# Attention and two MLPs on one core: weight copies on another queue, a denser operand split, and another pace of small work

## The chip, the cores and the metric

The kernel runs on one core of a Trainium2 chip. The metric is the device time of one execution in microseconds (us). TensorE (PE) multiplies, with its weight loads shown as PEld; VectorE (DVE) and ScalarE (ACT) do the elementwise work; GpSimd (POOL) and SyncE (SP) issue most of the transfers. Each engine runs its instructions in the order in which the program emits them.

## The reference

All data is float32. Softmax attention with a tanh cap over 4 batches, 12 heads, 448 tokens and head dimension 64 gives x (1792 x 768). A first MLP follows, then a second, gated one with two more products:

```
scores = cap * tanh(q k^T / 8 / cap);  attn = exp(scores - max) / sum
x = concat_heads(attn v)                       # 1792 x 768
x = square(relu(x @ w_in)) @ w_out             # 768 -> 2048 -> 768
h = ((x @ w1) * (x @ w2)) @ w3                 # 768 -> 1024 -> 1024
out = h @ w_out2                               # 1024 -> 768
```

The MLP weights come as float64 words, are narrowed on the chip, and are split into a high and a low part so that a product is three TensorE products: high by high, high by low, low by high.

## The kernel before, in words

**Attention (lines 393 to 713).** One loop, `for u in range(NU + 10)`, with `NU` = 84, emits everything. Each u below 84 is one unit: a 128-key slice of a pair of heads p (24 pairs, 7 units for two pairs). At an even u two units get their scores (`emit_qk`, tile `sc`) and `tanh`; `emit_exp` works on unit u-1, `emit_sum` adds unit u-4 into the denominators on DVE, and at an odd u `emit_pv` multiplies units u-5 and u-4 with v (tile `pv`). A table `later` says at which u a pair's `pv` is copied to `acc` (`evacuate`, line 515: pair 21 at u = 83, pair 22 at 87, pair 23 at 89), at which u its denominators are summed by TensorE (`emit_den`: pairs 20 and 21 at u = 83, pairs 22 and 23 at 91) and stored (`store_den`, line 520: u = 85 and 93).

**Weights beside the attention.** `w_piece` (line 561) is a generator, advanced once per u, that narrows and splits one piece of a weight. The eight "w0" pieces belong to the first MLP's first block; two steps after its low part is formed (line 80), such a piece is copied from SBUF to DRAM (`w0_d`, shown as `w_d`) by two transfers (line 580). `w_products` multiplies w3 with the last weight on TensorE; `w_store` sends the result out (line 610). At the first even u at which all of that is emitted, u = 84, the loop closes the weights' SBUF pool `wq`. The x operands (`xs[0]`, `xs[1]`, shown as x0h, x0l, x1h, x1l) are allocated in the same place; an operand waits only for the old tile it overlaps. Still at u = 84, three raw weight pieces are fetched and the eight w0 pieces read back (line 687), all on SP's queue.

**The hand-over.** `side` holds the generator `splits()`: for batch 0, then batch 1, `split_x` (line 273) makes in seven steps the high parts on ACT (line 280) and the low parts on DVE (line 80). It is advanced once per u. After batch 0 is split, each odd u takes one step of `fill`, which is `first_unit`: `front` for two 128-column blocks of w_in (18 products each, with relu, square and split on ACT and DVE), then `back` (six outputs). What is left of `side` and `fill` when the loop ends is emitted then:

```python
            advance(side)
            advance(norms)
        assert not w_open
        while side:
            advance(side)
        for _ in fill:
            pass
```

`normalise` (line 286, in the list `norms`, a step per u) divides a group of pairs by its denominators: it reads the stored denominators back (`dt`), forms reciprocals on DVE, stores them (`rec_d`), spreads them over partitions (`spread`, two transfers per pair into `bs`, line 303) and multiplies `acc` (line 311). For the last batch the last group is pairs 22 and 23.

**First MLP (lines 866 on).** 16 units of `front` and `back`, all products on TensorE, with weight conversion beside them. Batch 3's operand is split in the third unit and first used by the fourth.

**Second MLP.** 16 steps s, eight per pair of batches. `front2` (line 783) makes seven products p(0) to p(6) and combines them on DVE (lines 799, 802); `back2` (line 826) makes 12 outputs y and adds each to `acc` on DVE (line 842). The order in a step is the first half of `front2` (p(0) to p(3)), half of the previous `back2`, the rest of `front2`, the other half. Small work, the sums and splits of operands, waits in the list `duties` and is emitted by `tick(n)`, n items at a time: `tick(2)` after each p(j), `tick(1)` after each y. At s = 2 and s = 6 sums for the second pair are queued (16 and 3 items), at s = 7 its six operand splits (42 items: three high parts on ACT, three low parts on DVE and one empty item each).

Of the kernel before, what the change touches and what calls it, by code (L numbers as in the profile page):

```python
# [9 lines left out]
F32 = mybir.dt.float32  # L10
# [11 lines left out]
def tile_kernel(ctx, tc, q, k, v, cap, w_in, w_out, w1, w2, w3t, wo2, out):  # L22
# [31 lines left out]
    GD = 2  # L54
# [230 lines left out]
    def normalise(b, n0, n1, lags):  # L285

        rows = slice(2 * n0, 2 * n1)
        dt_ = stat.tile([128, 4 * GD * S // 128], F32, name="dt", bufs=2)[:, :2 * (n1 - n0) * S // 128]  # L290
        POOL.dma_start(out=dt_, in_=den_d[b][rows].rearrange("h s -> (h s)").rearrange("(p f) -> p f", p=128))
        for _ in range(lags[0]):
            yield
        DVE.scalar_tensor_tensor(out=dt_, in0=dt_, scalar=1e-9, in1=dt_, op0=ALU.mult, op1=ALU.add)
        DVE.reciprocal(out=dt_, in_=dt_)
        POOL.dma_start(out=rec_d[b][rows].rearrange("h s -> (h s)").rearrange("(p f) -> p f", p=128), in_=dt_)
        rs = {}

        def spread(n):
            if n < n1:  # L300
                rs[n] = cv.tile([128, 2, HW], F32R, name="bs", bufs=2).bitcast(F32).rearrange("p t n -> p (t n)")[:, :S]
                for j in range(2):
                    POOL.dma_start(out=rs[n][j * D:(j + 1) * D], in_=rec_d[b][2 * n + j].partition_broadcast(D))

        spread(n0)
        spread(n0 + 1)
        for n in range(n0, n1):
            for _ in range(lags[1] if n == n0 else lags[2]):
                yield
            a = acc[b][:, n, :]  # L310
            DVE.tensor_tensor(out=a, in0=a, in1=rs.pop(n), op=ALU.mult)
            normal.add((b, n))
            spread(n + 2)
# [75 lines left out]
    with ExitStack() as actx:  # L389
# [125 lines left out]

        def evacuate(p):
            b, hp = divmod(p, NP)
            DVE.tensor_copy(acc[b][:, hp, :], pvs.pop(p))

        def store_den(p):  # L520
            b, g, n = den_group(p)
            if p % NP // 2 == g + n - 1:
                stg = ap_.tile([128, S], F32, name="stg", bufs=1)
                DVE.tensor_copy(stg, dens.pop(b))
                for i in range(4):
                    POOL.dma_start(out=den_d[b].rearrange("(n i) s -> n i s", i=4)[g:g + n, i, :],
                                   in_=stg[32 * i:32 * i + n])
                lags = (6, 4, 3) if b < B - 1 else (7, 3, 1) if n == GD else (4, 3, 1)
                norms.append(normalise(b, 2 * g, 2 * (g + n), lags))
# [30 lines left out]
        def w_piece(n):  # L560
            kind, i, z = wsrc[n]
            raw = wraw.pop(n)
            if kind == "wo":
                x = block() if i < 5 else wq.tile([128, 2, HW], F32R, name=f"wo{i}{z}")
                parts = [x[:, 0, :], x[:, 1, :]]
            else:
                nj = raw.shape[-1] // 128
                tiles = [wq.tile([128, 3, 128], F32R, name=f"w3{s}", bufs=W3)[:, :nj, :] for s in "hl"]
                parts = [x.rearrange("p a c -> p (a c)") for x in tiles]
            g = narrow(raw, *parts, on=ACT if n >= ON_POOL and n % 2 else DVE, first=POOL if n < ON_POOL else ACT, pool=wq)  # L570
            next(g)
            w_fetch(n + 3)
            for _ in range(LAG):
                yield
            yield from g
            yield
            yield
            if kind == "w0":
                for s, x in enumerate(parts):
                    POOL.dma_start(out=w0_d[i, z, :, s, :], in_=x.bitcast(F32))  # L580
                w3_done.add(wsrc[n])
            else:
                w_ready[wsrc[n]] = parts if kind == "wo" else tiles
# [68 lines left out]
        for u in range(NU + 10):  # L652
            if u < NU and u % 7 in (1, 4):
                load_v(what(u)[0] + 1)
            if 0 <= u - 1 < NU:
                emit_exp(u - 1)
            if u % 2 == 0:
                if u < NU:
                    for x in (u, u + 1):
                        emit_qk(x)  # L660
                    for x in (u, u + 1):
                        emit_tanh(x)
                if w_open:
                    todo = -(-products_left // max((W_END - u) // 2, 1)) if u > W_EVEN else 4
                    for _ in range(todo):
                        x = next(wprod, None)
                        if not x:
                            break
                        products_left -= 1
                    if products_left <= 0:  # L670
                        for _ in wprod:
                            pass
                    if products_left <= 0 and not w_full and not chains:
                        wctx.close()
                        xp = ctx.enter_context(tc.tile_pool(name="x0", bufs=1, side="right", reuse_waits="tile"))
                        for b in range(EARLY):
                            xs[b] = [xp.tile([128, NP, S], F32R, name=f"x{b}{s}") for s in "hl"]
                        new_gtiles(xp)
                        rtiles.extend(cv.tile([128, S], F32, name="cvx", bufs=6) for _ in range(2))
                        w_open = False  # L680
                        fill = first_unit(spare_bank)
                        for _ in range(3):
                            fetch_next()
                        for i in range(2 * FC):
                            halves = [block() for _ in range(2)]
                            for z, x in enumerate(halves):
                                SP.dma_start(out=x.bitcast(F32), in_=w0_d[i, z])
                            wts[i] = [w for x in halves for w in columns(x)]
                        side.append(splits())
            else:  # L690
                w_store()
                if split_done:
                    next(fill, None)
                for x in (u - 5, u - 4):
                    if 0 <= x < NU:
                        emit_pv(x)
                for f in later.pop(u, ()):
                    f()
            for f in later.pop(u, ()):
                f()  # L700
            if w_open and u > 1 and wnext < len(wsrc) and wnext < min(u, W_FAST) * W_RATE[0] + max(u - W_FAST, 0) * W_RATE[1] and w_may_start(wnext):
                chains.append(w_piece(wnext))
                wnext += 1
            advance(chains)
            if 0 <= u - 4 < NU:
                emit_sum(u - 4)
            advance(side)
            advance(norms)
        assert not w_open
        while side:  # L710
            advance(side)
        for _ in fill:
            pass

# [68 lines left out]
    def front2(s):  # L783

        pair = s // NM
        ws = wblk.pop(s)
        ps = [ps_h.tile([128, 512], F32, name="h")[:, :S] for _ in range(7)]
        p1, u2, u3 = (cv.tile([128, S], F32, name="bt", bufs=3) for _ in range(3))
        u4 = spare[1]

        def p(j):
            assert (pair, ORDER[j]) in there
            products(ps[j], ws[j], *place(pair, ORDER[j]))
            if s == NM - 1 and j < 6:
                operand(1, ("B11", "T2", "T3", "B21", "T4", "B22")[j])
            tick(2)

        def add(t, j, u):
            DVE.tensor_tensor(out=t, in0=ps[j], in1=u, op=ALU.add)  # L799

        def gate(j, x, y):
            DVE.tensor_tensor(out=x, in0=x, in1=y, op=ALU.mult)  # L802
            gh, gl = (t[:, s % 2, :] for t in gtiles[j])
            ACT.activation(gh, x, AF.Copy)  # L804
            late.append((gl, x, gh))

        p(0)
        ACT.activation(p1, ps[0], AF.Copy)
        flush()
        p(1)  # L810
        add(u2, 1, p1)
        p(2)
        add(u3, 2, u2)
        p(3)
        add(u4, 3, u3)
        add(u2, 3, u2)
        yield
        p(4)
        add(p1, 4, p1)
        p(5)  # L820
        add(u3, 5, u3)
        gate(0, p1, u3)
        p(6)
        add(u2, 6, u2)
        gate(1, u2, u4)
        yield

    def back2(s):
# [3 lines left out]
        for half in range(2):  # L832
            for j, o in product(range(2), range(half * KB, (half + 1) * KB)):
# [8 lines left out]
                    DVE.tensor_tensor(out=a, in0=y, in1=a, op=ALU.add)  # L842
                if o == half * KB + 1:
                    flush()
                tick(1)
                if m == NM - 1:
                    SP.dma_start(out=out[o * 128:(o + 1) * 128, b * S:(b + 1) * S], in_=a)
            yield
# [117 lines left out]
```

## Time and profile before

| what | value |
|---|---|
| runs of before | 1062.25, 1063.03, 1065.13 us; median 1063.03 us |
| the profiled execution | 1064.73 us; its span 1062.8 us |
| PE busy | 1036.2 us, 97% of the span |
| DVE, ACT, POOL busy | 785.3, 535.2, 198.8 us |
| chain that ended last | PE 86%, DVE 8%, ACT 3%, DMA 1% |

Busy time is a share of the whole span; a stage is read from the rows of its own stretch. Times in rows count from the span's start. In the timeline a row gives start, length, engine, line, output and input; brackets give the idle time just before it and what ended it, as far as the profile can infer. The matmul rows overlap: the time between two starts is the pace, not the length of one.

### The profile page before, as it was taken

How to read it: one execution, taken by the hardware profiler on the slowest of the kernel's cores; microseconds unless marked ns; L12 is line 12 of the kernel's file. 1: busy time of each engine (PE TensorE's matmuls, PEld its weight loads, DVE VectorE, ACT ScalarE, POOL GpSimd, SP SyncE). 2: the span in 40 equal slices, each digit the busy share in tenths (PEclk: the TensorE clock that was granted, in tenths of full speed). 3: DMA queues.
4: the chain of work that ended last, by engine and by line, in shares of the span. 5: the costliest groups of instructions: out<-in, count | busy, mean ns of one | idle time of the engine just before them, and what ended most of it. 6: DMA issues, size and time to landing. Idle time of an engine off the chain costs nothing.

```text
span 1062.8 us, 14544 instructions
## 1 busy us (share of the span) xinstructions
PE 1036.2 (97%) x5136; PEld 844.9 (79%) x5136; DVE 785.3 (74%) x1485; ACT 535.2 (50%) x946; POOL 198.8 (19%) x360
## 2 busy tenths in 40 slices
PE   7999999997999999999999999999999999999998
PEld 2333555554899999999999999999989997999997
DVE  5999988766576878888788787567386678456666
ACT  7899988873776565555666555441311022300100
POOL 3222223324101011111111101002211322131110
PEclk9999999998999999999999999999999999999999
DMA  6667666663245565655656555126554567566443
GB/s 207 180 176 217 192 191 199 206 212 103 77 117 175 172 174 180 191 182 167 179 178 193 179 166 161 45 57 182 166 177 149 175 211 224 163 206 193 137 149 119
DMA packets 74216, 178.69 MB, mean 168 GB/s; under 512 B 10368, under 2 KB 25760, under 8 KB 74144
## 3 DMA queue, kind: packets, MB, share of 16 engines
q0 software_dynamic: 36992, 97.01, 28.9%
q1 hardware_dynamic: 37008, 80.76, 25.9%
q8 instruction: 40, 0.66, 0.3%
q14 instruction: 32, 0.26, 0.1%
q10 hardware_dynamic: 144, 0.00, 0.0%
HBM read 137.45 MB, written 40.28 MB: 167 GB/s over the span
## 4 chain that ended last, share of the span: by engine, by line
PE 86%; DVE 8%; ACT 3%; DMA 1%; issue 1%; POOL 0%; SPq 0%; DVEq 0%
PE h L320 13%; PE h L318 13%; PE h L319 13%; PE y L318 10%; PE y L319 10%; PE y L320 10%; PE sc L438 3%; PE pv L487 3%; PE h L596 2%; PE h L598 2%; PE h L597 2%; DVE sum L468 1%; ACT pt L458 1%; DVE acc L842 1%; ACT pt L454 1%
## 5 line engine op out<-in xcount | busy, mean ns | idle before, releaser
L319 PE MATMUL y<-gl,wb 128*128 128x448 f32 x372 | 136.4, 367 | 0.0
L320 PE MATMUL y<-gh,wb 128*128 128x448 f32 x372 | 136.3, 367 | 0.0
L318 PE MATMUL y<-gh,wb 128*128 128x448 f32 x372 | 136.3, 366 | 0.0
L799 DVE TENSOR_TENSOR bt<-h,bt 128x448 f32<-128x448 f32 x96 | 59.8, 623 | 91.8 <-PE h L320 75.5
L804 ACT ACTIVATE gh<-bt 128x448 fp32r<-128x448 f32 x32 | 18.5, 578 | 205.0 <-DVE bt L802 205.0
L371 DVE TENSOR_TENSOR acc<-y,acc 128x448 f32<-128x448 f32 x168 | 99.4, 621 | 22.3 <-PE y L320 21.4
L228 POOL DMA_DIRECT2D wc_d<-bs x72 | 38.5, 535 | 333.1 <-DVE cvx L120 158.1
L842 DVE TENSOR_TENSOR acc<-y,acc 128x448 f32<-128x448 f32 x168 | 94.4, 618 | 0.0
L454 ACT ACTIVATE pt<-sc,scl 128x896 f32<-128x896 f32 x84 | 80.5, 1009 | 23.2 <-PE sc L438 17.1
L458 ACT ACTIVATE pt<-pt,capt 128x896 f32<-128x896 f32 x84 | 86.5, 1042 | 0.0
L774 POOL DMA_DIRECT2D wb<-wc_d x112 | 59.4, 544 | 114.2 <-PE h L320 91.0
L438 PE MATMUL sc<-rq,rk 64*128 64x448 f32 x288 | 68.6, 588 | 10.3 <-ACT pt L454 5.3
L318 PEld LDWEIGHTS y<-gh,wb 128*128 128x128 f32 x372 | 69.9, 188 | 6.1
L319 PEld LDWEIGHTS y<-gl,wb 128*128 128x128 f32 x372 | 69.9, 188 | 6.0
L320 PEld LDWEIGHTS y<-gh,wb 128*128 128x128 f32 x372 | 69.9, 188 | 5.9
L318 PE MATMUL y<-gh,raw 128*128 128x448 f32 x192 | 71.6, 373 | 2.4 <-ACT x0h L759 0.8
L80 DVE TENSOR_TENSOR gl<-gr,gh 128x448 fp32r<-128x448 f32 x62 | 38.5, 621 | 47.4 <-ACT gh L354 47.4
L116 ACT ACTIVATE cvx<-raw 128x384 int32<-128x384 uint32 (+1 forms) x136 | 73.4, 540 | 0.0
L113 ACT ACTIVATE cvx<-raw 128x384 f32<-128x384 f32 x124 | 66.8, 539 | 7.3 <-DMA raw<-w_in 3.9
L319 PE MATMUL y<-gl,raw 128*128 128x448 f32 x192 | 70.4, 367 | 0.0
L320 PE MATMUL y<-gh,raw 128*128 128x448 f32 x192 | 70.4, 366 | 0.0
L320 PE MATMUL h<-x2h,wb 128*128 128x448 f32 x192 | 70.2, 366 | 0.0
(166 smaller groups left out, 2527.1 us busy)
## 6 DMA issues: line engine op xcount, KB each, us to landing
wb<-wc_d POOLq DMA_DIRECT2D x112, 384.0 KB, 5.9
wc_d<-bs POOLq DMA_DIRECT2D x72, 384.0 KB, 3.0
raw<-w_in SPq DMA_DIRECT2D x32, 384.0 KB, 3.9
raw<-w_out SPq DMA_DIRECT2D x32, 384.0 KB, 3.9
raw<-w SPq DMA_DIRECT2D x32, 384.0 KB, 3.8
raw<-wc_d POOLq DMA_DIRECT2D x32, 384.0 KB, 3.4
raw<-w3t SPq DMA_DIRECT2D x16, 384.0 KB, 4.2
raw<-wo SPq DMA_DIRECT2D x16, 384.0 KB, 3.3
```

Of the source, the lines that this page charges most:

```text
L113: ACT.activation(a, upper, AF.Copy, scale=2.0 ** -112)
L116: ACT.activation(r, words[:, :, 0], AF.Copy, scale=2.0 ** -29)
L318: PE.matmul(ps, wh, xh[:, i, :], start=start and i == 0, stop=False)
L319: PE.matmul(ps, wh, xl[:, i, :], start=False, stop=False)
L320: PE.matmul(ps, wl, xh[:, i, :], start=False, stop=(i == n - 1))
L371: DVE.tensor_tensor(out=a, in0=y, in1=a, op=ALU.add)
L438: PE.matmul(sc[:, j, :S], rk[r, 128 * t:128 * t + 128], rq[r, :], start=True, stop=True, tile_position=(j * D, 0))
L454: ACT.activation(pt, units[u], AF.Tanh, scale=scl)
L458: ACT.activation(units[u], units[u], AF.Exp, scale=capt)
L774: POOL.dma_start(out=x, in_=wc_d[s % NM, j])
L799: DVE.tensor_tensor(out=t, in0=ps[j], in1=u, op=ALU.add)
L842: DVE.tensor_tensor(out=a, in0=y, in1=a, op=ALU.add)
```

## The change

Five edits. The w0 copies are issued by SP instead of POOL. The copies of the last three pairs' `pv` (21, 22, 23) go to ACT. From u = 86 on, `side` is advanced three steps at a time. `tick` emits three items after each p(j) (was two) and, after each y, one item if o is odd and none otherwise (was one). In the last batch's last group, half of the denominators' stores and half of the spreading transfers are issued by SP.

```diff
@@ normalise / spread
-                    POOL.dma_start(out=rs[n][j * D:(j + 1) * D], in_=rec_d[b][2 * n + j].partition_broadcast(D))
+                    (SP if j and b == B - 1 and n1 == NP else POOL).dma_start(out=rs[n][j * D:(j + 1) * D], in_=rec_d[b][2 * n + j].partition_broadcast(D))
@@ evacuate
-            DVE.tensor_copy(acc[b][:, hp, :], pvs.pop(p))
+            a = acc[b][:, hp, :]
+            (ACT.activation(a, pvs.pop(p), AF.Copy) if p >= NPAIR - 3 else DVE.tensor_copy(a, pvs.pop(p)))
@@ store_den
-                    POOL.dma_start(out=den_d[b].rearrange("(n i) s -> n i s", i=4)[g:g + n, i, :],
+                    (SP if i % 2 and b == B - 1 and n < GD else POOL).dma_start(out=den_d[b].rearrange("(n i) s -> n i s", i=4)[g:g + n, i, :],
@@ w_piece
-                    POOL.dma_start(out=w0_d[i, z, :, s, :], in_=x.bitcast(F32))
+                    SP.dma_start(out=w0_d[i, z, :, s, :], in_=x.bitcast(F32))
@@ attention loop, and after it
-            advance(side)
+            advance(side, 3 if u >= NU + 2 else 1)
@@ front2, p(j)
-            tick(2)
+            tick(3)
@@ back2
-                tick(1)
+                tick(o % 2)
```

## Rows read from the trace of the kernel before

**Rows 1.** Stretches: length, busy (count) of PE, PEld, DVE, ACT, POOL, clock, DMA, GB/s.
```profile
20.00:60.00 40.00, 37.21 (x194) 12.58 (x190) 38.33 (x69) 37.14 (x48) 12.29 (x12) 1.00 0.61 179
...
250.00:260.00 10.00, 6.65 (x19) 4.69 (x20) 7.95 (x15) 0.00 (x0) 1.83 (x4) 0.66 0.10 33
...
300.00:500.00 200.00, 200.00 (x982) 184.10 (x981) 158.89 (x318) 124.23 (x257) 20.84 (x39) 1.00 0.58 176
```

**Rows 2.** What PE waited for over the whole span: total, times, longest.
```profile
PE sc L438 <- ACT pt L454: 5.3, 5, 1.5
PE den L513 <- DVE sum L468: 5.3, 3, 4.6
...
PE y L318 <- ACT x0h L759: 0.8, 1, 0.8
PE y L318 <- DVE acc L842: 0.7, 2, 0.5
```

**Rows 3.** Timeline of PE at the attention's end.
```profile
245.44 2.48 PE L487 MATMUL pv<-pt,rv 128*64 128x448 f32 x12
...
253.35 1.71 PE L513 MATMUL den<-sum,sel 128*32 128x448 f32 x4 [4.55 <-DVE sum L468]
254.99 0.74 PE L318 MATMUL sc<-x0h,wb 128*128 128x448 f32 x1
...
264.39 0.37 PE L318 MATMUL sc<-gh,wb 128*128 128x448 f32 x1
...
267.07 0.47 PE L319 MATMUL sc<-gl,wb 128*128 128x448 f32 x1 [0.19 <-DVE gl L80]
```

**Rows 4.** Timeline of DVE at the attention's end.
```profile
233.01 0.56 DVE L80 TENSOR_TENSOR w3l<-cvt,w3h 128x384 fp32r<-128x384 f32 x1 [1.70 <-ACT w3h L136]
...
244.67 0.62 DVE L524 COPY stg<-den 128x448 f32<-128x448 f32 x1 [1.58 <-PE den L513]
248.31 0.63 DVE L80 TENSOR_TENSOR x0l<-acc,x0h 128x448 fp32r<-128x448 f32 x1 [3.02 <-DMA w_d<-w3h]
248.86 1.08 DVE L468 TENSOR_TENSOR sum<-pt 128x896 f32<-128x896 f32 x1
...
251.69 0.61 DVE L518 COPY acc<-pv 128x448 f32<-128x448 f32 x1
252.22 1.07 DVE L468 TENSOR_TENSOR sum<-sum,pt 128x896 f32<-128x896 f32 x1
...
255.89 0.61 DVE L80 TENSOR_TENSOR x1l<-acc,x1h 128x448 fp32r<-128x448 f32 x1
```

**Rows 5.** Timeline of POOL before and after the last copies.
```profile
238.29 1.03 POOL L303 DMA_DIRECT2D bs<-rec_d  x2 [7.11 <-DVE acc L311]
...
242.88 0.54 POOL L610 DMA_DIRECT2D wp_d<-cvt  x1 [1.95 <-ACT cvt L609]
243.41 0.54 POOL L580 DMA_DIRECT2D w_d<-w3h  x1
...
265.29 0.56 POOL L291 DMA_DIRECT2D dt<-den_d  x1 [2.00 <-DMA den_d<-stg]
```

**Rows 6.** Timeline of ACT at the hand-over.
```profile
243.41 2.90 ACT L280 ACTIVATE x0h<-acc 128x448 fp32r<-128x448 f32 x6
```

**Rows 7.** Timeline of SP's queue at the hand-over.
```profile
225.29 1.28 SPq L93 DMA_DIRECT2D raw<-w_in  x3
226.66 22.32 SPq L687 DMA_DIRECT2D wb<-w_d  x8
```

**Rows 8.** Time from issue to landing, 224 to 260 us: transfers, KB, median us.
```profile
wb<-w_d SPq DMA_DIRECT2D x8, 384.0 KB, 6.2
```

**Rows 9.** Timeline of DVE in the first MLP: batch 3's last reciprocals.
```profile
283.41 0.24 DVE L295 RECIPROCAL dt<-dt 128x14 f32<-128x14 f32 x1
```

**Rows 10.** Timeline of PE in the second MLP, the waits of steps 2 and 7.
```profile
782.21 0.47 PE L318 MATMUL y<-gh,raw 128*128 128x448 f32 x1 [0.49 <-DVE acc L842]
...
886.15 0.44 PE L318 MATMUL y<-gh,raw 128*128 128x448 f32 x1 [0.77 <-ACT x0h L759]
```

More of the change, by code (lines that the diff above doesn't have):

```diff
@@ L710, in tile_kernel @@
         while side:
-            advance(side)
+            advance(side, 3 if u >= NU + 2 else 1)
         for _ in fill:
```

## The prediction

> **What bounds the kernel now.** I read first the table by stretch: through the MLPs PE is busy for all of its time, 982 products in 200 us or 0.204 us each at a granted clock of 1.00, the 2.4 GHz level, while between 250 and 260 us it was busy for 6.65 of 10 us and the clock stood at 0.66 [rows 1]. So time is to be had only where PE stands still, and the list of its waits shows where: 4.6 us in one piece before the last denominators, and in the second MLP 0.8 and 0.7 us before y products [rows 2]. Nearly everything is at the attention's end.
>
> The timeline there reads backwards. PE ends its last pv products at 245.44 + 2.48 = 247.92, but the second half of the denominators starts only at 253.35, after 4.55 us of idling; then the first MLP's 36 front products take from 254.99 to 264.39, 9.40 us where 36 x 0.204 = 7.33 would do, because after that idle stretch the granted clock is at the lower level (0.66 as a mean over the stretch, 1.2 GHz in part of it) [rows 1, 3]. PE waited for DVE's last sum (252.22), and DVE had itself stood still for 3.02 us before its first low part x0l, released at 248.31 by the copy of w3h to DRAM [rows 4]. x0l lies where that w0 piece lay. The piece's low part was finished at 233.01 + 0.56 = 233.57 [rows 4], but POOL issued the copy only at 243.41: it had been stuck until 238.29 behind a spreading transfer that waited 7.11 us for DVE, and then behind the store of a weight product at 242.88 [rows 5]. So a copy whose data was there lay 9.8 us in a queue.
>
> **Part by part.**
>
> *Copies on SP.* Counting the loop's steps, the last two copies come on SP's queue after the attention's loads and ahead of the three raw fetches and the eight read-backs that SP had reached at 225.29 and 226.66 [rows 7]. So SP waits there for the low part, 233.57, and issues at once. From issue to landing it took 248.31 - 243.41 = 4.9 us [rows 4, 5]; landing at 238.5, or with the slower 6.2 us of the read-backs at 239.8 [rows 8], is well before DVE wants to write x0l. **The 3.02 us wait goes.** What SP holds back is fetched later: three raws and eight blocks, 11 x 0.39 MB, start at 233.6 instead of 225.3. At the 179 GB/s of 20 to 60 us [rows 1] the raws and the first two blocks (1.97 MB) need 11.0 us, to 244.6, before the first front product; all 4.3 MB need until 257.6, when the last blocks are about due. I cost this at nothing, covered by the attention's own products; if the cover fails, 1 to 2 us. The other six copies join SP's loads of q, k, v and raws: between nothing (the loads are ahead of their use) and 0.39 MB / 179 GB/s = 2.2 us each, 13.2 us in all, if each load behind them came late and PE paid. I take nothing: the nearest rows, the read-backs, land in 6.2 us [rows 8], and raws are fetched three pieces ahead. POOL's 16 x 0.54 us of issue are off the path, since POOL itself waits [rows 5].
>
> *pv copies on ACT and the denser split.* DVE is next: its denominator copy at 244.67 waits for PE and stays [rows 4]; its cost is the 0.55 between two starts (248.31 to 248.86, [rows 4]), so x0l starts at 245.22. ACT makes the six high parts from 243.41 in 2.90 us [rows 6]; with one pv copy ahead of them (0.6, as DVE's 0.61) and one among them they end near 247.5, ahead of the low parts. In before, DVE needs from 248.31 to 255.89 for six low parts, its last sums and two pv copies, 7.58 us [rows 4]; the pv copies at 0.53 each (251.69 to 252.22) go to ACT, which has nothing to do between 250 and 260 us [rows 1], and 6.52 us are left. **x0 is complete at 251.74.** The three-step pace adds no work; it emits front's first half four u earlier, so that front stands ahead of the denominators on PE.
>
> *PE.* It is free at 247.92 and follows the low parts (one to four are there by 249.7), so the first 18 products end 0.4 us after the last low part, at 252.2; 18 more at 0.204 end at 255.9. In before that point is 264.39 [rows 3]: **8.5 us earlier**, of which about 2.1 is the clock. No gap that I count is over 1.1 us; between 20 and 60 us, where PE stood still for 2.79 us in several pieces, the granted clock stayed 1.00 [rows 1]. From there to the first product with the second gl is a chain of relu, square and split that doesn't change: 267.07 - 264.39 = 2.68 us [rows 3]. In it PE has four products of 0.2 us, so the denominators, now after front and 1.71 us long at the worst [rows 3], fit into its idle time: nothing, or 0.9 us for half of them.
>
> *Last denominators on two queues.* They now end 1 to 2 us later, while the reciprocals that need them, at 283.41 [rows 9], move 8.5 us forward with PE, to 274.9. The read-back issued at 265.29 [rows 5], even 1.7 us later, at 267.0, leaves 7.9 us, more than the 6.2 us of a large block [rows 8]. I cost the two queues at nothing; the stores and spreads shorten a chain that isn't late, by the 0.54 us of issue of each of four transfers [rows 5].
>
> *Pace of small work.* A step emits 7 x 3 + 6 = 27 items instead of 14 + 12 = 26. At s = 2, up to the first y of the second half, DVE gets seven sums and low parts instead of eight, 0.53 us less, which removes the 0.49 us wait at 782.21 [rows 10]: 0.5 us. At s = 7, DVE's order up to the third y after p(6) is the same in both kernels (one item and two gl parts), so the 0.77 us at 886.15 [rows 10] stays. Bounds: at best all 1.5 us of these waits [rows 2]; at worst a loss of 2 us, should the seven items added to a front2 (about three on DVE, 0.62 each) hold up its sums. I take 0.5, the nearer row.
>
> **Sum.** 8.5 + 0.5 = 9.0 us from the profiled execution's 1064.73 us gives 1055.7. That execution is 1.7 us above the median of the runs, 1063.03, so the forecast is 1063.0 - 9.0 = **1054.0 us**. PE is full in the MLPs [rows 1], so nothing hands the gain back there.
>
> **The rivals.**
>
> *The wait for the copy stays* (10%): SP's copies land late, or another tile is what x0l waits for. Then x0l starts at 248.31 as now, x0 is complete 6.52 us later, at 254.83, front ends at 255.2 + 3.7 = 258.9, 5.4 us earlier than now: with the 0.5, 1063.0 - 5.9 = 1057.1 us. For it: all transfers share the same engines; against it: 11 us between the piece and its need. The Trainium skill, DMA: Bandwidth & Descriptors (Issuing engines are not separate DMA queues), says that transfers of all issuing engines run interleaved on the same 16 DMA engines, and that issuing from several saves only the sequencer's time, usually small. By that the move would give nothing and this rival would be the result; the trace agrees on the transfers (4.9 us by POOL), but the sequencer's time here is the 9.8 us.
>
> *The second MLP pays* (6%): 2 us lost instead of 0.5 won: 1063.0 - 6.5 = 1056.5 us.
>
> *Loads behind copies on SP, slower* (5%): six copies hold the q, k, v and raw loads behind them by 2.2 us each and PE pays 13.2 us: 1063.0 - 9.0 + 13.2 = 1067.2 us. It decides from the point at which a load lands after its first use; before that it costs nothing. For it: a single in-order queue; against it: loads run ahead by units. If half of that is paid, 1060.6 us, the change is within the noise (5%).
>
> **How the numbers follow.** A run tells 0.3%, 3.2 us, from no change. The forecast has 74%; it and the first two rivals are faster by more: 0.90. Same 0.05, slower 0.05. The range goes down to all of the second MLP's waits (10.0 us won, 1053.0) less 1.8 us for scatter (the lowest run is 0.8 under the median) and for a DVE chain 1 us shorter, 1051.2; up to the first rival without the second MLP's gain (1057.6) and 1 us of scatter, 1058.6.
>
> **What would show it.** Right: w_d copies issued by SP near 233.6; no idle time before the first x0l, at about 245.2; the first front product near 248 and back's first product near 256, at a clock of 1.00; no 4.55 us wait for den. In the second MLP no wait near step 2, the one at step 7 kept. Wrong: x0l still released by a transfer, PE waiting for rk, rq, rv or a raw's conversion before 240 us, for wb at front, or for x3 in the first MLP's fourth unit.

## The result, and the profile after

The changed kernel takes **1054.53 us** in the median (1054.25 to 1054.68) against 1063.03 us before, a ratio of 0.9915 with a 95% interval of 0.9893 to 0.9938. The forecast was 1054.0 us. The profiled execution is 1054.53 us long, its span 1052.8 us; before they were 1064.73 and 1062.8 us.

First the stretches at the hand-over, columns as in [rows 1]: PE is busy for 9.15 us between 250 and 260 us (6.65 before) and the granted clock is 1.00 (0.66 before). The MLPs are as full as they were.

```profile
240.00:250.00 10.00, 10.00 (x59) 5.28 (x58) 5.40 (x9) 5.58 (x12) 2.62 (x5) 1.00 0.99 383
250.00:260.00 10.00, 9.15 (x45) 6.57 (x44) 7.72 (x15) 6.59 (x13) 1.12 (x2) 1.00 0.02 5
...
300.00:500.00 200.00, 200.00 (x982) 184.02 (x981) 158.58 (x318) 119.60 (x248) 21.42 (x40) 1.00 0.58 177
```

SP's queue in the changed kernel: the last copy's two transfers go out at 233.52 and 234.11, in the moment in which their data is there; the raw fetches and the read-backs follow.

```profile
233.52 0.32 SPq L581 DMA_DIRECT2D w_d<-w3h  x1
234.11 0.32 SPq L581 DMA_DIRECT2D w_d<-w3l  x1
234.48 2.23 SPq L93 DMA_DIRECT2D raw<-w_in  x3
236.76 5.55 SPq L688 DMA_DIRECT2D wb<-w_d  x8
```

DVE's timeline answers to [rows 4]: the first x0l follows the copy of the denominators without idle time, and the last two start at 251.16, so x0 is complete at 252.23, where x1l begins.

```profile
233.52 0.56 DVE L80 TENSOR_TENSOR w3l<-cvt,w3h 128x384 fp32r<-128x384 f32 x1 [1.70 <-ACT w3h L136]
...
245.18 0.62 DVE L525 COPY stg<-den 128x448 f32<-128x448 f32 x1 [3.72 <-PE den L513]
245.72 0.61 DVE L80 TENSOR_TENSOR x0l<-acc,x0h 128x448 fp32r<-128x448 f32 x1
...
250.15 1.08 DVE L468 TENSOR_TENSOR sum<-sum,pt 128x896 f32<-128x896 f32 x1
251.16 1.15 DVE L80 TENSOR_TENSOR x0l<-acc,x0h 128x448 fp32r<-128x448 f32 x2
252.23 2.21 DVE L80 TENSOR_TENSOR x1l<-acc,x1h 128x448 fp32r<-128x448 f32 x4
```

PE's timeline answers to [rows 3]: front starts as the last pv products end (248.4), has one listed pause, 0.51 us, for the low part behind the last sum, and takes the denominators only at 256.74.

```profile
245.95 2.48 PE L487 MATMUL pv<-pt,rv 128*64 128x448 f32 x12
248.36 0.47 PE L318 MATMUL sc<-x0h,wb 128*128 128x448 f32 x1
...
251.82 0.47 PE L319 MATMUL sc<-x0l,wb 128*128 128x448 f32 x1 [0.51 <-DVE x0l L80]
...
256.74 0.96 PE L513 MATMUL den<-sum,sel 128*32 128x448 f32 x8
257.63 0.47 PE L318 MATMUL sc<-gh,wb 128*128 128x448 f32 x1
...
259.32 0.47 PE L319 MATMUL sc<-gl,wb 128*128 128x448 f32 x1 [0.19 <-DVE gl L80]
...
266.00 0.37 PE L318 MATMUL h<-x1h,wb 128*128 128x448 f32 x1
```

The list of PE's waits over the whole span, as in [rows 2]: the 4.6 us for the denominators are gone, the 0.8 us before a y are still there, and 0.7 us for DVE's adds have become 0.2.

```profile
PE sc L438 <- ACT pt L454: 5.1, 5, 1.5
...
PE y L318 <- ACT x3h L760: 0.8, 1, 0.8
PE den L513 <- DVE sum L468: 0.7, 2, 0.4
...
PE sc L319 <- DVE x0l L80: 0.5, 1, 0.5
...
PE y L318 <- DVE acc L843: 0.2, 1, 0.2
```

**Where the time came from.** Three landmarks on PE's timeline cut each profile: the end of the last pv products (the attention), the first product with x1 (the hand-over), the start of the last y product (the MLPs). The table has them for every kernel of this study, all by the same rows. The medians come from four sessions; the ratios below are to the runs of before in the same session (1063.22 us for e1 to e4, 1063.91 for e5 to e8, 1063.06 for e9 to e11). The stages of a kernel come from its one profiled execution.

| kernel | pv end, us | hand-over, us | MLPs, us | median of the runs, us |
|---|---|---|---|---|
| before | 247.92 | 25.83 | 783.81 | 1063.03 |
| before, second profile (e11) | 247.87 | 23.98 | 783.60 | 1063.03 |
| e1, before with copies on SP alone | 248.84 | 20.03 | 783.88 | 1059.43 |
| e3, before with the new pace alone | 247.79 | 25.04 | 782.27 | 1061.41 |
| **changed** | 248.43 | 17.57 | 781.94 | 1054.53 |
| changed, second profile (e10) | 248.04 | 17.56 | 781.88 | 1054.85 |
| e2, changed with copies on POOL | 247.80 | 20.95 | 781.94 | 1056.87 |
| e4, changed with one queue for the denominators | 248.20 | 17.57 | 782.17 | 1054.63 |
| e5, changed with the slow split | 248.34 | 19.49 | 781.75 | 1056.55 |
| e6, changed with pv copies on DVE | 248.26 | 18.09 | 782.20 | 1055.27 |
| e7, changed, small work all in front2 | 247.91 | 17.57 | 781.98 | 1054.93 |
| e8, changed, split ahead of the sums | 248.64 | 16.77 | 782.29 | 1053.95 |
| e9, e8 and a finer pace | 248.56 | 16.77 | 781.10 | 1053.27 |

Between the first two profiles of before and changed: attention 0.51 us longer, hand-over 8.26 us shorter, MLPs 1.87 us shorter, and 0.4 us less behind the last product (1062.8 - 1057.56 = 5.24 us before, 1052.8 - 1047.94 = 4.86 us after): 10.0 us of span. No run shows where these 0.4 us come from; the stretch takes 5.2 us in before, e11 and e3 and 4.5 to 4.9 us in the ten other profiles.

### The profile page after: what moved, and what is told of

Same layout as the page of the kernel before. It is cut to its first block, busy times and chain, and to the rows that moved or that the text cites. A ratio compares the mean times of both kernels' runs of the same rounds, so it can differ in the third digit from the quotient of the medians.

```text
span 1052.8 us, 14553 instructions
## 1 busy us (share of the span) xinstructions
PE 1032.6 (98%) x5136; PEld 842.9 (80%) x5136; DVE 783.7 (74%) x1482; ACT 536.7 (51%) x949; POOL 188.8 (18%) x340
## 4 chain that ended last, share of the span: by engine, by line
PE 86%; DVE 7%; ACT 4%; DMA 2%; issue 1%; DVEq 0%
PE h L318 14%; PE h L320 14%; PE h L319 14%; PE y L318 11%; PE y L319 11%; PE y L320 11%; PE sc L438 3%; PE pv L487 3%; PE h L597 2%; PE h L599 2%; PE h L598 2%; ACT pt L458 2%; ACT pt L454 1%; DVE sum L468 1%; DVE sum L474 1%; DVE acc L843 1%
## 5 line engine op out<-in xcount | busy, mean ns | idle before, releaser
L438 PE MATMUL sc<-rq,rk 64*128 64x448 f32 x288 | 68.6, 588 | 10.2 <-ACT pt L454 5.1
L319 PE MATMUL h<-x2l,wb 128*128 128x448 f32 x192 | 70.1, 365 | 0.0
```

The costliest lines, as they stand in the source:

```text
L319: PE.matmul(ps, wh, xl[:, i, :], start=False, stop=False)
L438: PE.matmul(sc[:, j, :S], rk[r, 128 * t:128 * t + 128], rq[r, :], start=True, stop=True, tile_position=(j * D, 0))
```

## The experiments

The theory is the prediction's: a copy late in POOL's queue holds DVE, DVE holds PE, and the idle PE loses its clock. The first rival is that the wait is worth only its own 3 us and the other edits make the rest. Second, for the MLPs: the prediction's 0.5 us against the 1.9 us that the traces show. Third: the queues of the last denominators matter.

**e1, the copies alone.** Edit on the kernel before:

```diff
-                    POOL.dma_start(out=w0_d[i, z, :, s, :], in_=x.bitcast(F32))
+                    SP.dma_start(out=w0_d[i, z, :, s, :], in_=x.bitcast(F32))
```

> The kernel before with one edit, the w0 copies on SP's queue. Theory (the copy's wait in POOL's queue started a chain: DVE idle, PE idle, lower clock): x0l starts near 245.2 instead of 248.31, DVE's 7.58 us until x0 is complete stay (two pv copies among them), so x0 is complete near 252.8, front's 36 products end near 256.9 instead of 264.39, with the granted clock at 1.00: 7.5 us faster than before, nearly all of the hand-over's gain. Rival (the wait is worth only itself, the denser split and the pv copies make the rest): 3.0 us faster, PE still idle for over 1.5 us before the denominators and the clock still down after it.

Measured: 1059.43 us, ratio to before 0.9968 (0.9957 to 0.9979). The hand-over is 5.80 us shorter than in the first profile of before, between the two expectations; against the second profile, e11, it is 3.95 us. By their medians the runs gain 3.8 us (2.2 to 4.6), nearer to the rival's 3.0 than to the theory's 7.5. PE's timeline of e1:

```profile
248.77 0.95 PE L513 MATMUL den<-sum,sel 128*32 128x448 f32 x4
251.16 0.95 PE L513 MATMUL den<-sum,sel 128*32 128x448 f32 x4 [1.44 <-DVE sum L468]
...
259.53 0.37 PE L318 MATMUL sc<-gh,wb 128*128 128x448 f32 x1
261.12 0.47 PE L319 MATMUL sc<-gl,wb 128*128 128x448 f32 x1 [1.22 <-DVE gl L80]
```

PE's idle time before the denominators falls from 4.55 to 1.44 us and the granted clock between 250 and 260 us is 1.00: the chain to DVE and to the clock is as the theory has it, its size is not. What I had left out is the order on PE. In this kernel the denominators stand ahead of front; they end near 252.1, and 36 products of 0.204 us then end at 259.5, however early x0 is. x0 was complete at 253.7, as expected (252.8, with a start of the stage that was 0.9 us later here).

**e2, everything but the copies.** The reverse edit on the changed kernel:

```diff
-                    SP.dma_start(out=w0_d[i, z, :, s, :], in_=x.bitcast(F32))
+                    POOL.dma_start(out=w0_d[i, z, :, s, :], in_=x.bitcast(F32))
```

> The changed kernel with the w0 copies back on POOL's queue. Theory of overlapping gains (the denser split puts front ahead of the denominators, so PE is not idle long enough for the clock to fall even with the late copy): x0l starts near 248.3, x0 is complete near 254.8, front ends near 258.9, 2.5 to 3.1 us slower than the changed kernel, clock 1.00. Rival (the copies' queue is the whole of it): over 7 us slower than the changed kernel, PE idle for about 4 us and the clock down as in the kernel before.

Measured: 1056.87 us, ratio 0.9949 (0.9933 to 0.9965); the hand-over is 3.4 us longer than in the changed kernel. DVE's and PE's timeline and the stretch:

```profile
247.60 0.63 DVE L80 TENSOR_TENSOR x0l<-acc,x0h 128x448 fp32r<-128x448 f32 x1 [2.43 <-DMA w_d<-w3h]
```
```profile
251.10 0.47 PE L319 MATMUL sc<-x0l,wb 128*128 128x448 f32 x1 [1.94 <-DVE x0l L80]
```
```profile
250.00:260.00 10.00, 8.90 (x40) 7.18 (x40) 7.72 (x14) 3.52 (x8) 0.00 (x0) 0.83 0.06 21
```

The wait for the copy is back, on the same instruction and transfer, so the queue is what removed it. But PE, which now has front's first product ahead, idles for 1.94 us in one piece, and the clock still falls in part of the stretch (0.83): the hand-over is 0.3 to 0.9 us longer than the 2.5 to 3.1 us expected without that. The whole execution is only 2.2 to 2.3 us longer by the medians, since in e2's profile the attention ended 0.63 us earlier and the stretch behind the last product was 0.35 us shorter. Each half alone gives 5.8 us (e1) and 4.9 us (e2, 25.83 - 20.95), together 8.26: they overlap, by 2.4 us. Against e11's 23.98 the same numbers are 3.95, 3.03 and 6.41, an overlap of 0.6 us: its size hangs on what the gap cost in before.

**e5, the split at its old pace**, on the changed kernel, in both places:

```diff
-            advance(side, 3 if u >= NU + 2 else 1)
+            advance(side)
```

> The changed kernel with one step of the split per u again, so that TensorE takes the last denominators ahead of front. Theory (order on PE, not work, is what the pace changes): DVE reaches its last sum about 0.5 us earlier, at 250.1, the denominators end near 251.1, and all 36 front products come after that, ending near 258.5 instead of 256.6; the 2.7 us chain behind front has no denominators left to hide. So 1.9 us slower than the changed kernel. Rival (the pace is worth nothing, the low parts set the end either way): within 0.3 us of the changed kernel.

Measured: 1056.55 us, ratio 0.9932 (0.9920 to 0.9944); hand-over 19.49 - 17.57 = 1.92 us longer. Two waits come back: the one ahead of the denominators, and the whole of the chain behind front, in which the changed kernel runs the denominators:

```profile
PE sc L319 <- DVE gl L80: 1.4, 2, 1.2
PE den L513 <- DVE sum L468: 0.9, 1, 0.9
```

**e6, the pv copies on DVE**, on the changed kernel:

```diff
-            (ACT.activation(a, pvs.pop(p), AF.Copy) if p >= NPAIR - 3 else DVE.tensor_copy(a, pvs.pop(p)))
+            (ACT.activation(a, pvs.pop(p), AF.Copy) if p >= NPAIR else DVE.tensor_copy(a, pvs.pop(p)))
```

> The changed kernel with all pv copies on DVE again. Theory: of the three copies only pair 22's stands ahead of low parts of x0 (before the last sum); it delays the fifth and sixth low part and so front by its 0.53 us, pair 21's falls into DVE's idle time and pair 23's behind x0: 0.5 us slower than the changed kernel. Rival, the prediction's term: two copies count, 1.07 us slower.

Measured: 1055.27 us, ratio 0.9917 (0.9903 to 0.9930); hand-over 0.52 us longer, and the wait of front for x0l is 1.0 us where it was 0.5. One copy counts, not two. From kernel to kernel the hand-over goes down: 25.83 before, 20.03 with the copies (e1), 19.49 with the pv copies on ACT too (e5, which also has the two queues, worth nothing by e4), 17.57 with the split's pace.

**e3, the pace of the second MLP alone**, on the kernel before:

```diff
-            tick(2)
+            tick(3)
@@ back2
-                tick(1)
+                tick(o % 2)
```

> The kernel before with only the pace of small work in the second MLP changed. Theory from the two traces (starts of the same instructions in both kernels drift apart by 0.53 us at step 2 and by 1.2 us at step 7, where before had pauses of 0.25 us ahead of many y products that no list of waits shows): 1.8 us faster than before. Rival, the prediction's own term: 0.5 us faster, only the listed wait of step 2 gone.

Measured: 1061.41 us, ratio 0.9984 (0.9974 to 0.9995), 1.6 to 1.8 us less than the 1063.0 to 1063.2 of before. The interval, 0.5 to 2.8 us, holds both expectations; the stage tells them apart. The MLPs take 782.27 us instead of 783.81 (783.60 in the second profile of before): 1.3 to 1.5 us. Over all profiles the MLPs take 783.60 to 783.88 us in the three with the old pace and 781.75 to 782.29 in the eight with the new one (e7 and e9 have their own), 1.7 us less in the mean. Most of it is step 7, where the start of the same DVE instruction in steps 7 and 8 shows the step's length. In the kernel before:

```profile
872.37 0.62 DVE L799 TENSOR_TENSOR bs<-h,bt 128x448 f32<-128x448 f32 x1 [0.68 <-PE h L320]
...
902.85 0.62 DVE L799 TENSOR_TENSOR bs<-h,bt 128x448 f32<-128x448 f32 x1 [1.20 <-PE h L320]
```

and in the changed kernel:

```profile
864.04 0.62 DVE L800 TENSOR_TENSOR bs<-h,bt 128x448 f32<-128x448 f32 x1 [0.15 <-PE h L320]
...
893.33 0.62 DVE L800 TENSOR_TENSOR bs<-h,bt 128x448 f32<-128x448 f32 x1 [1.20 <-PE h L320]
```

30.48 us become 29.29, in e3 too (871.08 to 900.37). In before, five y products between 886 and 895 us start 0.38 to 0.49 us after the product ahead of them, where 0.2 is the pace; in the changed kernel two start late, by 0.45 and 0.33. The list of waits has none of these. DVE's timeline shows what they wait on. Between p(6) of step 7 and the next step DVE adds 18 y, with small work among them. The first and the last of these adds, and the item behind them, in before:

```profile
882.76 0.62 DVE L842 TENSOR_TENSOR acc<-y,acc 128x448 f32<-128x448 f32 x1
...
895.54 1.69 DVE L842 TENSOR_TENSOR acc<-y,acc 128x448 f32<-128x448 f32 x3
897.14 1.70 DVE L80 TENSOR_TENSOR x3l<-acc,x3h 128x448 fp32r<-128x448 f32 x3
```

and in the changed kernel:

```profile
874.43 0.62 DVE L843 TENSOR_TENSOR acc<-y,acc 128x448 f32<-128x448 f32 x1
...
885.60 1.69 DVE L843 TENSOR_TENSOR acc<-y,acc 128x448 f32<-128x448 f32 x3
887.19 0.63 DVE L80 TENSOR_TENSOR x0l<-gr,x0h 128x448 fp32r<-128x448 f32 x1
```

DVE has no listed wait in either stretch (busy for all of 13.90 us from 882.7 to 896.6 in before, and for all of 12.80 us from 874.4 to 887.2 in changed). It is 14.38 us long with seven low parts among the adds, 12.76 us with four: three low parts of 0.53 us. DVE, not PE, sets the pace of these y products.

**e4, one queue for the last denominators**, on the changed kernel:

```diff
-                    (SP if j and b == B - 1 and n1 == NP else POOL).dma_start(...)
+                    POOL.dma_start(...)
-                    (SP if i % 2 and b == B - 1 and n < GD else POOL).dma_start(...)
+                    POOL.dma_start(...)
```

> The changed kernel with the last denominators' stores and spreads all on POOL's queue again. Theory (that chain has slack of several us before batch 3's operand is needed): no difference from the changed kernel, under 0.3 us. Rival (the chain is near its limit once PE is 8 us earlier): PE waits for x3 in the first MLP's fourth unit and the kernel is 1 to 2 us slower than the changed one.

Measured: 1054.63 us, ratio 0.9929 (0.9915 to 0.9943), hand-over 17.57 us as in the changed kernel, and no new wait. The chain had room, as costed.

**e7, all small work in front2**, on the changed kernel:

```diff
-            tick(3)
+            tick(4)
@@ back2
-                tick(o % 2)
```

> The changed kernel with the small work of the second MLP wholly in front2: four items after each p(j), none after a y. Theory (DVE has room beside the 1.85 us products of front2 and none beside back2's 0.61 us ones): the 0.78 us wait at step 7 shrinks to 0.25 us or less and the small pauses of step 7 go, 0.7 to 1.2 us faster than the changed kernel. Rival (front2's sums on DVE are held up by four items, TensorE waits for its banks there): as slow or slower than the changed kernel, with new waits of h products.

Measured: 1054.93 us, ratio 0.9914 (0.9900 to 0.9927); the MLPs take 781.98 us, no change. The small pauses of step 7 are gone, but its seventh y still waits (0.70 us, 0.78 in the changed kernel), and waits of 0.5 us now stand before its fifth y and before a y of step 2 (PE's timeline of e7):

```profile
773.84 0.47 PE L318 MATMUL y<-gh,raw 128*128 128x448 f32 x1 [0.51 <-DVE acc L843]
...
875.62 0.47 PE L318 MATMUL y<-gh,raw 128*128 128x448 f32 x1 [0.54 <-DVE acc L843]
...
877.80 0.44 PE L318 MATMUL y<-gh,raw 128*128 128x448 f32 x1 [0.70 <-ACT x0h L760]
```

DVE shows why: in the last items behind p(6) a low part waits for its high part on ACT, and front2's last sum stands behind it, so the y adds begin late.

```profile
873.21 0.63 DVE L80 TENSOR_TENSOR x1l<-acc,x1h 128x448 fp32r<-128x448 f32 x1 [0.58 <-ACT x1h L760]
873.75 0.62 DVE L800 TENSOR_TENSOR bt<-h,bt 128x448 f32<-128x448 f32 x1
```

So the rival held in its second half: not h, but y products paid.

**e8, the split ahead of the sums**, on the changed kernel:

```diff
+            if u >= NU + 2:
+                advance(side, 3)
             if 0 <= u - 4 < NU:
                 emit_sum(u - 4)
-            advance(side, 3 if u >= NU + 2 else 1)
+            if u < NU + 2:
+                advance(side)
```

> The changed kernel with the split of x ahead of the attention's last sums on DVE from u = 86 on. Theory (front still waits 0.51 us for a low part that stands behind the last sum, and follows the low parts with pauses): all six low parts are ready by 249, front runs without a pause from 248.4 and ends 0.9 us earlier; the denominators, then 1 us later, still find their sums done: 0.9 us faster than the changed kernel. Rival (the sums become late, the denominators hold up back's products on PE): no gain, a wait of den for the sum in place of the wait for x0l.

Measured: 1053.95 us, ratio 0.9904 (0.9891 to 0.9918); the hand-over is 0.80 us shorter, front runs without a pause, and no wait for the sums takes its place (PE's waits between 240 and 300 us):

```profile
PE sc L319 <- DVE gl L80: 0.2, 1, 0.2
PE sc L318 <- ACT gh L354: 0.2, 1, 0.2
```

**e9, e8 with a finer pace**, beside **e10** and **e11**, the changed kernel and the kernel before once more. The edit on e8:

```diff
-            tick(3)
+            tick(4 if j < 4 else 3)
@@ back2
-                tick(o % 2)
+                tick(o % 2 if j or not half else 0)
```

> The changed kernel with the split ahead of the last sums (0.8 us, as measured alone) and small work moved from the first three y of back2's second half into the first half of front2 (four items after p(0) to p(3), three after p(4) to p(6)). Theory (at step 7 the seventh y waits for the third add, which stands behind one low part; low parts before p(4) are free): the 0.78 us wait at step 7 falls to about 0.25 us and the 0.2 us at step 2 goes, 0.5 to 0.8 us from the first instructions of the second MLP to its end, with the split 1.3 to 1.6 us faster than the changed kernel. Rival (DVE's backlog only moves, as with all small work in front2): the second MLP takes as long as in the changed kernel, 0.8 us faster from the split alone.

> The changed kernel once more, beside the two others: 1054.5 us, as measured before, under either theory. It gives a second look at the attention's length (end of the last pv products at 247.8 to 247.9 us with copies on POOL, 247.9 to 248.8 with copies on SP). Theory (a transfer's landing near 105 us, ahead of the first copy, makes the difference by chance): anywhere between 247.8 and 248.8. Rival (copies on SP lengthen the attention): above 248.2.

> The kernel before once more: 1063 us under either theory. Theory (chance): the last pv products end anywhere between 247.8 and 248.8 us. Rival (copies on SP lengthen the attention): 247.8 to 248.0. Between there and the first product with x1 it should again take 25 to 26 us with a granted clock below 0.9 in the stretch behind 250 us.

Measured: e9 1053.27 us, ratio to before 0.9907 (0.9894 to 0.9921); e10 1054.85 us, 0.9921 (0.9908 to 0.9935); e11 1063.03 us, 0.9994 (0.9983 to 1.0006). e9 is below the changed kernel by 1.6 us beside it, 0.8 us each from the hand-over (16.77) and the MLPs (781.10); its wait at step 7 is 0.4 us instead of 0.8:

```profile
PE y L318 <- ACT x3h L763: 0.4, 1, 0.4
```

e11's hand-over is 23.98 us, not 25 to 26, with this stretch and wait:

```profile
250.00:260.00 10.00, 7.39 (x28) 6.05 (x29) 7.22 (x14) 0.95 (x2) 2.02 (x4) 0.83 0.07 25
```
```profile
PE den L513 <- DVE sum L468: 3.9, 1, 3.9
```

The same instructions, but 3.9 us of idling instead of 4.55, and more of the stretch at the higher clock (0.83 as a mean instead of 0.66).

On the attention: with copies on POOL the last pv products end at 247.79 to 247.92 us (four profiles), with copies on SP at 247.91 to 248.84 (nine). e10's 248.04 is below the rival's 248.2 but above all four of POOL's. Part of it is a spreading transfer that DVE waits for near 105 us, 0.84 us in before and 1.49 in changed, ahead of the first copy (113.7), so the copies' traffic can't have made it:

```profile
104.32 0.62 DVE L311 TENSOR_TENSOR acc<-acc,bs 128x448 f32<-128x448 f32 x1 [0.84 <-DMA bs<-rec_d]
```
```profile
105.14 0.63 DVE L311 TENSOR_TENSOR acc<-acc,bs 128x448 f32<-128x448 f32 x1 [1.49 <-DMA bs<-rec_d]
```

In e10 that wait is only 0.42 us and the end still 248.04. The products for the denominators, which stand in every profile, show where the time goes:

```profile
123.67 0.96 PE L513 MATMUL den<-sum,sel 128*32 128x448 f32 x8
```
```profile
124.22 0.96 PE L513 MATMUL den<-sum,sel 128*32 128x448 f32 x8
```

From this start (before, then changed) to the end of the last pv products all thirteen profiles take 124.19 to 124.26 us, though the copies of seven of the eight pieces, from 138 us on, lie in that stretch. So what differs lies ahead of it, where only the first piece is copied, near 113.6 us. In seven of the nine kernels with copies on SP this start is late, by 19.06 to 19.10 us after DVE's multiplication with the late spread (105.14 in changed), with no listed wait on DVE between. In the two others, e7 and e10, the stretch from the denominators near 103 us to those near 124 is as long as with copies on POOL (20.43 and 20.44 us, against 20.44 to 20.51), and e10's 0.2 us are there at 103.41 already (103.08 to 103.21 with copies on POOL). So the copies on SP cost the attention nothing in these traces. Why the spread near 105 us is later in seven of the nine (1.41 to 1.90 us of waiting) than in the four (0.84 to 1.20) stays open.

## Why the prediction was right, and where it was off

- **Copies on SP.** As worked out: issue at 233.52 and 234.11 (233.6 forecast), no wait before x0l, x0l at 245.72 (245.2 in a stage that began 0.5 us later). e2 shows that the wait comes back with the queue. From issue to landing the last copies took about 2 us on SP (medians 1.9 and 2.2), not the 4.9 of POOL's, but their start 10 us earlier is what counts: with 4.9 us they would land by 239.0. The read-backs, at 383 GB/s between 240 and 250 us, held nothing on PE; the 257.6 us at which I had the last of them land, by a rate of 179 GB/s, was too late, for between 250 and 260 us only 5 GB/s still move. One wait took the old one's place on ACT, 2.16 us before x1h, put down to a read-back, in e8 to the store of a weight product, whose source lies in the same old pool; it costs nothing, since DVE reaches x1l later.
- **x0 complete.** Forecast 251.74, with the stage 0.51 us later 252.25; measured 252.23.
- **PE.** 8.5 us earlier forecast, measured 8.26 from the end of pv to the first product with x1. The chain behind front is 259.32 - 256.64 = 2.68 us, as it was, with the denominators inside it; 256.64 is 0.2 us behind front's last start, 256.44. No gap over 1 us, clock 1.00. e5 shows that the place of front ahead of the denominators is worth 1.92 us of this, and e6 that the pv copies are worth 0.52, not the 1.06 us of two copies; the forecast's sum ran through one chain and so didn't need these shares.
- **Last denominators on two queues.** Costed at nothing; e4 shows nothing.
- **Second MLP: the term that was mis-sized.** I took 0.5 us; it is 1.9 us between the two profiles, 1.3 to 1.5 in e3. Over all profiles it is 1.7 us in the mean. Step 2 gave its 0.5 (the waits there are 0.2 instead of 0.7) and the 0.77 us wait of step 7 stayed (0.78 at 877.82), both as argued. What failed is the rest of step 7, which I put at nothing because I priced this part by the list of waits alone: behind that wait DVE is full, and four low parts instead of seven among its adds shorten the step by 1.19 us. The list holds no pause of 0.25 us, and there were five. Between the two profiles the gain also passed the bound of 1.5 us that I had put on this part.
- **The six other copies.** Costed at nothing; PE's waits in the attention show no new one for q, k, v or a raw; the one for the first q, 4.9 us at the kernel's start, is 4.8 in before. The attention was 0.5 us longer, but not by the copies; see above.
- **The sum and the median.** Against its own execution the change gave 10.2 us (1064.73 to 1054.53), not 9.0; against the median 8.5. The forecast 1054.0 came within 0.5 us because two errors cancelled: the second MLP gave more, and the profiled execution of before had paid more in the gap than an execution near the median (e11, 1063.15 us: 1.85 us less in the hand-over, of it 0.7 in idle time), so that its gain could not be taken from the median in full. That these two met is luck.
- **The rivals.** The wait for the copy did not stay; the Trainium skill's sentence on issuing engines (DMA: Bandwidth & Descriptors, Issuing engines are not separate DMA queues) holds for the transfers, which ran beside others at up to 383 GB/s on average, but what the move saved was not the issue itself, 0.54 us on POOL and 0.32 on SP: it was the 9.8 us for which the copy stood behind others in POOL's order. The second MLP did not pay. Nothing of the 13.2 us of late loads showed.

## What to carry to other kernels

When an operand waits for a transfer, look at when that transfer's data was ready and when its queue issued it; if a long wait in the queue lies between (here 9.8 us, behind a spread that waited for another engine), move the issue to a queue that has nothing late ahead of it. When several edits shorten one hand-over, cost them as one chain with the order on the last engine in it, because in the profiles they gave 5.8 and 4.9 us alone and 8.3 together. Price small work by the busy time of the engine that carries it in that stretch (DVE had no idle time in 14.4 us here), not by the list of waits alone.

## What the runs showed that was not expected

The gap costs a varying amount: three profiles of the same code (before, e11, e3) took 25.83, 23.98 and 25.04 us over the hand-over. Part of that is idle time (4.55, 3.87 and 4.92 us before the denominators), part the clock: from the start of the second half of the denominators to the first product with gh it is 11.04, 9.91 and 9.92 us, and 8.37 in e1, where the clock stayed at 1.00. So the lower clock cost 2.7, 1.5 and 1.5 us, and the longest gap was not the one that cost most. Without the gap the scatter is smaller too: the 58 runs of the kernel before spread from 1060.17 to 1066.26 us, the eight of the changed kernel and its second copy from 1054.11 to 1055.04 us. That the gap makes the scatter is not shown run by run, but e2, which still idles 1.94 us at a mean clock of 0.83, spreads over 3.1 us in six runs, and e1, at a clock of 1.00, over 1.5 us in eight.
